# Eight transfers of whole rows in place of four of 32 partitions for the last half of an output

## The chip, the cores and the metric

The kernel runs on one core of a Trainium2 chip. The metric is the device time of one execution in microseconds (us), the median of several runs. The profile is of one further execution; its span goes from the first to the last instruction.

## The reference

Two blocks, one behind the other, all in float32.

```python
# attention: q, k, v are (4, 8, 768, 64), proj is (64, 6)
mask = q_bucket[:, :, :, None] == k_bucket[:, :, None, :]    # buckets: signs of q @ proj and k @ proj as a number
scores = where(mask, scale * q @ k.T, -1e9); attn = softmax(scores); x = attn @ v
x = x.transpose(0, 2, 1, 3).reshape(3072, 512)               # tokens x model
# feed-forward: w_in is (512, 2048), w_out is (2048, 512)
h = x @ w_in
g = h * (1 / (1 + exp(-1.702 * h)))
out = g @ w_out                                              # 3072 x 512
```

## The kernel before

The attention comes first (lines up to about 540), pair of heads by pair of heads, and leaves x transposed in the tile xT. The feed-forward block (`feed_forward`, from L698) works on three groups of 1,024 tokens (`sb`), each of two halves of XT = 512 tokens, themselves of two parts of TH = 256. Both matrix products are done by a scheme of seven products of half-size matrices in place of eight, so sums of quarters are made by DVE and POOL beside TensorE's products. The first product's results g lie in a DRAM buffer, `g_dram`; the second product reads them back into `raw_g` (and a second buffer in `s_in`) for 3 x 7 = 21 steps (`steps_out`), in the order `OUTER = (1, 2, 6, 7, 5, 3, 4)` for each group.

One such step is `product_of_halves` (its products at L1078, the sums of its results at L1083): seven smaller products again. Between them it calls `after(0)`, `after(1)` and so on, by which the loop over the steps places other work: the order of every engine's instructions is written out by hand, and the engines keep it.

A result c has the output's features on the partitions. `turned` (L1058) transposes it in blocks of 32 x 32 on DVE, quarter by quarter (q = 0 to 3), into the tile `ys[j]` of 128 partitions x 16 blocks x 128 floats; j says which 512 tokens of the group. After this, partition 32a + t of block b holds the output row of token 32b + t, columns 128a to 128a + 127. Quarters 0 and 2 of the final step complete blocks 0 to 7 (the first 256 tokens), quarters 1 and 3 blocks 8 to 15.

`written` (L1060 to L1065) brings blocks to the output in DRAM. It issues four transfers, one for each a: 32 partitions of `ys[j]`, the blocks asked for, 128 floats each; on the DRAM side rows of 512 floats, of which column block a is written. `queues` lists the engines that issue, in turn. `loader` is [SP]; for the last pieces ACT is added, so that SP issues a = 0 and 2 and ACT a = 1 and 3.

The last of the 21 steps (`final`) has its own order of products (L1090 on) and its own list of what is placed between them (L1271): quarter 1 after the fourth product, quarter 3 and the write of half 1 (`write[1]`) after the fifth, quarter 0, and at the very end, behind the last product, quarter 2, which transposes straight from the PSUM bank, and the write of half 0 (`write[0]`). `write` is built in L1269.

Behind the feed-forward block every engine loads a guard value (`largest`, L1312) and branches over a second version of the whole computation (the `tc.If` at L1315), which isn't taken here. SP waits for the completions of the outstanding transfers (L1315), and all engines drain and meet (L1348).

Of the kernel before, what the change touches and what calls it, by code (L numbers as in the profile page):

```python
# [19 lines left out]
P = 128  # L20
# [18 lines left out]
def kernel(  # L39
# [17 lines left out]
    nc = tc.nc  # L57

    loader = [nc.sync]
# [168 lines left out]
    XT = 512  # L228
# [469 lines left out]
    def feed_forward(tag, late=()):  # L698
# [9 lines left out]
        with ExitStack() as fctx:  # L708
# [306 lines left out]
            def inner_sums(at):  # L1015

                if at == 0:
                    w = w_quarters(OUTER[0])
                    return sums_a(nc.gpsimd, *w, wqs[LEFT[OUTER[0]]][:, 1, 0:F4, :])
                return sums_a(nc.gpsimd, *w_quarters(OUTER[at])) if at < len(OUTER) else []  # L1020
# [4 lines left out]
            def fetch(n):  # L1025
                sb, o = steps_out[n]
                parts = 1 if n + 1 == len(steps_out) else 2
                for h in range(parts):
                    cs = slice(h * FC // 2 // parts, (h + 1) * FC // 2 // parts)
                    loader[0].dma_start(out=raw_g[n % 2][:, cs], in_=g_dram[len(LEFT) * sb + RIGHT[o], :, cs, :])  # L1030
# [3 lines left out]
            def g_quarters(n):  # L1034
                if n not in g_tiles:


                    g_tiles[n] = wholes[4:6] if n == 1 else [
                        (st2 if n % 2 else gp).tile([P, F4, TH], F32, tag=t, name=t + "ab"[n % 2]) for t in ("t1", "t2")]
                    g_tiles[n] = g_tiles[n] + [gp.tile([P, F4, TH], F32, tag="t4", name="t4g")]  # L1040
                g = raw_g[n % 2]
                x = [g[:, F4 * k : F4 * (k + 1), TH * j : TH * (j + 1)] for k in range(2) for j in range(2)]
                return x + g_tiles[n]

            def g_sums(n):
                if n == len(steps_out):
                    return [lambda: None] * 4
                t1, d12, t2, t4 = sums_b(nc.vector, *g_quarters(n))
                return [t1, t2, d12, t4]

            ys = {}

            def turned(c, i, j, q0, q1, of=None):

                for q in range(q0, q1):
                    h, k = divmod(q, 2)
                    y = ys[j].rearrange("p b (d r) -> p r b d", r=4)[:, 2 * i + h, k * (TH // 32) : (k + 1) * (TH // 32), :]
                    nc.vector.transpose(y, (c[:, q] if of is None else of).rearrange("p (b t) -> p b t", t=32))  # L1058

            def written(sb, j, halves, queues):  # L1060
                first, last = halves[0] * TH, (halves[-1] + 1) * TH
                for a in range(4):
                    t0 = (2 * sb + j) * XT
                    dst = out[t0 + first : t0 + last, a * P : (a + 1) * P].rearrange("(b t) d -> t b d", t=32)
                    queues[a % len(queues)].dma_start(out=dst, in_=ys[j][32 * a : 32 * (a + 1), first // 32 : last // 32, :])  # L1065

            def product_of_halves(n, acc, after):

                sb, o = steps_out[n]
# [20 lines left out]
                if n + 1 == len(steps_out):  # L1090

                    a = product(1)
                    nc.scalar.copy(u, a)
                    b = product(3)
                    after(0)
                    product(6, onto=a)
                    nc.scalar.copy(v, a)
                    add(v, v, acc[:, 1])
                    add(c12, b, v)
                    after(1)  # L1100
                    p = product(5)
                    add(c12, p, c12)
                    add(c22, p, acc[:, 3])
                    after(2)
                    product(7, onto=a)
                    add(c22, a, c22)
                    add(a, a, acc[:, 2])
                    after(3)
                    corner()
                    after(4)  # L1110
                    product(4, onto=a)
                    after(5, a)
                    return m
# [62 lines left out]
            first = 2 * NESTED.stop  # L1176
# [12 lines left out]
            x = todo.pop(1, [])  # L1189
# [6 lines left out]
            for t in NESTED:  # L1196
                sb, at = divmod(t, MT // 2)
# [26 lines left out]
            for n in range(2 * NESTED.stop, 3 * MT):  # L1224
                sb, mt = divmod(n, MT)
# [13 lines left out]
                t = {3 * MT - 2: g_sums(0)[:1], 3 * MT - 1: g_sums(0)[1:]}.get(n, []) if n > 3 * MT - 3 else []  # L1239
# [8 lines left out]
            for n, (sb, o) in enumerate(steps_out):  # L1248
                final = n + 1 == len(steps_out)
                if 0 < n and n + 1 < len(steps_out):  # L1250
                    fetch(n + 1)

                if n in (2, 3, 5, 6):

                    nc.gpsimd.tensor_copy(mark, (g_quarters(n)[5] if n < 4 else ms[OUTER[n - 1]])[0:1, 0, 0:1])
                for f in {2: inner_sums(3), 3: inner_sums(4), 5: inner_sums(5) + inner_sums(6)[:2], 6: inner_sums(6)[2:]}.get(n, []):
                    f()
                later_sums = g_sums(n + 1)
                m = wholes[n % len(wholes)]

                def after(at, last=None):
                    if at == 0:
                        while pending:
                            pending.pop(0)()
                    todo = [[x] for x in later_sums] if n == 0 else [[], later_sums[0:1], later_sums[1:3], later_sums[3:]]
                    todo = todo[at] if not final else []
                    if n + 2 >= len(steps_out):
                        turns = [lambda q=q: turned(m, int(final), int(not final), q, q + 1, last if q == 2 else None) for q in range(4)]
                        write = [lambda x=(sb, int(not final), (h,), loader + [nc.scalar] * (final or h == 0)): written(*x) for h in range(2)]  # L1269
                        if final:  # L1270
                            todo = [[], last_sum, [turns[1]], [turns[3], write[1]], [turns[0]], [turns[2], write[0]]][at]  # L1271
                        elif at == 2:
                            todo = [later_sums[1], turns[1], turns[3], write[1]]
                        elif at == 3:
                            todo = [turns[2], turns[0], later_sums[2]]
                            pending.append(write[0])
                            last_sum.append(later_sums[3])
                    for f in todo:
                        f()

                acc = {6: 1, 7: 6, 2: 1, 3: 6, 4: 7}.get(o)
                if o == 3:
                    pending.pop(0)()
                ms[o] = product_of_halves(n, None if acc is None else ms[acc], after)

                def flat(x):
                    return x.rearrange("p q t -> p (q t)")

                if o == 5:
                    m5, m6, m7 = (ms[i] for i in (5, 6, 7))  # L1290
                    pending += [lambda a=m6, b=m5: nc.vector.tensor_tensor(flat(a), flat(a), flat(b), op=Alu.add),
                                lambda a=m5, b=m7: nc.vector.tensor_tensor(flat(a), flat(a), flat(b), op=Alu.add),
                                lambda a=m5: turned(a, 1, 1, 0, 4)]
                elif o in (2, 3) and n + 2 < len(steps_out):
                    pending.append(lambda a=ms[o], j=int(o == 3): turned(a, 0, j, 0, 4))
                    if o == 3:
                        pending.append(lambda sb=sb: written(sb, 1, (0, 1), loader))
                elif o == 4 and not final:
                    pending.append(lambda a=ms[4]: turned(a, 1, 0, 0, 4))
                    pending.append(lambda sb=sb: written(sb, 0, (0, 1), loader))  # L1300
                yield
# [50 lines left out]
```

## Time and profile before

| | before |
|---|---|
| median of 3 runs | 856.52 us (856.17 to 859.51) |
| the profiled execution | 856.59 us |
| its span | 854.7 us, granted TensorE clock 0.998 |
| PE busy | 846.2 us, 99% of the span |
| DVE, POOL, ACT busy | 698.8, 357.3, 345.0 us |
| transfers from y to the output | 32: 16 of 256 KB and 16 of 128 KB |
| last transpose into y | 847.94 to 848.57 us of the span |
| last four transfers to the output | issued from 848.60 us on |

The times within the profile are counted from the start of the span. PE is TensorE's matrix products, PEld its weight loads, DVE VectorE, ACT ScalarE, POOL GpSimd, SP the engine that only issues transfers and waits. A q behind an engine's name means its sequencer: issues, waits and branches. "out<-in" are the program's names. The DMA share is the busy share of the core's 16 DMA engines; a packet is one contiguous piece that one of them moves.

### The profile page before, as it was taken

How to read it: one execution, taken by the hardware profiler on the slowest of the kernel's cores; microseconds unless marked ns; L12 is line 12 of the kernel's file. 1: busy time of each engine (PE TensorE's matmuls, PEld its weight loads, DVE VectorE, ACT ScalarE, POOL GpSimd, SP SyncE). 2: the span in 40 equal slices, each digit the busy share in tenths (PEclk: the TensorE clock that was granted, in tenths of full speed). 3: DMA queues.
4: the chain of work that ended last, by engine and by line, in shares of the span. 5: the costliest groups of instructions: out<-in, count | busy, mean ns of one | idle time of the engine just before them, and what ended most of it. 6: DMA issues, size and time to landing. Idle time of an engine off the chain costs nothing.

```text
span 854.7 us, 13648 instructions
## 1 busy us (share of the span) xinstructions
PE 846.2 (99%) x5007; PEld 530.4 (62%) x5007; DVE 698.8 (82%) x1069; ACT 345.0 (40%) x549; POOL 357.3 (42%) x316
## 2 busy tenths in 40 slices
PE   9999999999999999999999999999999999999996
PEld 4444444444444444566666666545888888888885
DVE  4589999999999885788887788666998977897776
ACT  5866667777766654343444444433000000000000
POOL 4343333433433358996854476669664100000000
PEclk9999999999999999999999999999999999999999
DMA  5636654444553104436565536587844685467524
GB/s 130 94 55 108 109 92 85 85 86 89 119 100 76 48 26 139 157 114 234 196 220 222 222 147 222 196 280 261 291 164 158 203 251 189 163 209 243 192 107 101
DMA packets 160906, 132.10 MB, mean 155 GB/s; under 512 B 122656, under 2 KB 137664, under 8 KB 155584
## 3 DMA queue, kind: packets, MB, share of 16 engines
q1 hardware_dynamic: 152448, 106.89, 44.8%
q10 hardware_dynamic: 8384, 24.27, 8.2%
q8 instruction: 41, 0.67, 0.4%
q14 instruction: 33, 0.27, 0.1%
HBM read 79.69 MB, written 50.33 MB: 152 GB/s over the span
## 4 chain that ended last, share of the span: by engine, by line
PE 98%; ACT 0%; POOL 0%; DVE 0%; issue 0%; ACTq 0%; POOLq 0%; DVEq 0%
PE product L1078 30%; PE product L751 23%; PE ps L435 18%; PE av L468 15%; PE small L819 6%; PE product L819 3%; PE dn L489 1%; PE hash L411 1%; PE tp L369 1%; PE hash L376 0%; ACT c L764 0%; DVE v L767 0%; POOL kf L310 0%; ACT size L190 0%; DVE y L1058 0%
## 5 line engine op out<-in xcount | busy, mean ns | idle before, releaser
L436 ACT ACTIVATE e<-ps 128x768 f32<-128x768 f32 x192 | 151.2, 812 | 25.6 <-PE ps L435 23.1
L435 PE MATMUL ps<-qT,kT 64*128 64x384 f32 x768 | 155.1, 483 | 0.0
L443 POOL TENSOR_TENSOR acc<-e 128x768 f32<-128x768 f32 x32 | 51.8, 1619 | 193.9 <-ACT e L436 174.4
L468 PE MATMUL av<-e,v 128*32 128x385 f32 x1536 | 128.0, 487 | 0.0
L751 PE MATMUL product<-xT,w_in_sb 128*128 128x512 f32 x216 | 100.1, 593 | 0.1
L468 PEld LDWEIGHTS av<-e,v 128*32 128x32 f32 x1536 | 48.6, 109 | 76.2 <-issue 74.0
L435 PEld LDWEIGHTS ps<-qT,kT 64*128 64x128 f32 x768 | 68.0, 188 | 38.5 <-issue 38.4
L751 PE MATMUL product<-t_x,s_in 128*128 128x512 f32 x192 | 89.4, 592 | 0.0
L1114 ACT COPY u<-product 128x256 f32<-128x256 f32 x20 | 7.4, 372 | 158.1 <-PE product L1078 124.9
L751 PEld LDWEIGHTS product<-xT,w_in_sb 128*128 128x128 f32 x216 | 40.9, 190 | 36.4 <-issue 33.1
L435 PE MATMUL ps<-qf,kf 64*128 64x384 bf16 x384 | 62.9, 324 | 0.1
L444 POOL TENSOR_TENSOR acc<-acc,e 128x768 f32<-128x768 f32 x32 | 55.9, 1746 | 2.5
L751 PEld LDWEIGHTS product<-t_x,s_in 128*128 128x128 f32 x192 | 36.5, 190 | 29.6 <-issue 27.2
L449 DVE SCALAR_TENSOR_TENSOR acc<-e 128x768 f32<-128x768 f32 x32 | 47.7, 1490 | 5.1 <-ACT e L436 5.1
L767 DVE TENSOR_TENSOR u<-product,u 128x256 f32<-128x256 f32 (+1 forms) x60 | 28.5, 487 | 17.1 <-PE product L819 13.8
L435 PEld LDWEIGHTS <-kf 64*128 64x128 bf16 x384 | 19.0, 94 | 35.1 <-issue 6.8
L451 DVE TENSOR_TENSOR acc<-acc,e 128x768 f32<-128x768 f32 x32 | 34.3, 1072 | 3.3
L451 DVE TENSOR_TENSOR acc<-acc,acc 128x768 f32<-128x768 f32 x32 | 31.2, 974 | 6.3 <-POOL acc L444 3.2
L1078 PE MATMUL product<-raw_g,xT 128*128 128x256 f32 x152 | 35.1, 379 | 0.0
L222 POOL TENSOR_TENSOR u<-v,u 128x1024 f32<-128x1024 f32 (+1 forms) x11 | 23.8, 2164 | 21.9 <-ACT v L764 8.1
L767 DVE TENSOR_TENSOR v<-product,v 128x512 f32<-128x512 f32 x24 | 16.5, 689 | 19.4 <-PE product L751 19.4
L767 DVE TENSOR_TENSOR c<-small,c 128x256 f32<-128x256 f32 (+1 forms) x54 | 24.2, 462 | 9.2 <-PE small L819 9.1
(284 smaller groups left out, 1728.0 us busy)
## 6 DMA issues: line engine op xcount, KB each, us to landing
raw_g<-g_dram SPq DMA_DIRECT2D x20, 1024.0 KB
s_in<-g_dram SPq DMA_DIRECT2D x20, 1024.0 KB
g_dram<-c ACTq DMA_DIRECT2D x18, 512.0 KB
raw<-in_moe_w_out_dram ACTq DMA_DIRECT2D x16, 512.0 KB
raw<-in_moe_w_in_dram SPq DMA_DIRECT2D x15, 512.0 KB
v<-in_v_dram SPq DMA_DIRECT2D x32, 192.0 KB
k<-in_k_dram SPq DMA_DIRECT2D x60, 96.0 KB
q<-in_q_dram SPq DMA_DIRECT2D x60, 96.0 KB
```

The source lines that it names most:

```text
L222: return [lambda: eng.tensor_tensor(t1, b12, b11, op=Alu.subtract), lambda: eng.tensor_tensor(b12, b22, b12, op=Alu.subtract), lambda: eng ...
L435: nc.tensor.matmul(ps[:, j, 0:HS], a[hs, keys], m[hs, cols], start=not last, stop=last)
L436: nc.scalar.activation(es[c][:, kt, :, 0:HS], ps[:, :, 0:HS], Act.Exp, scale=1.0 / D**0.5)
L443: nc.gpsimd.tensor_tensor(acc, es[c][:, 0, :, 0:HS], es[c][:, 1, :, 0:HS], op=Alu.add)
L444: nc.gpsimd.tensor_tensor(acc, acc, es[c][:, 2, :, 0:HS], op=Alu.add)
L449: nc.vector.scalar_tensor_tensor(acc, e[0], T * TINY, e[1], op0=Alu.add, op1=Alu.add)
L451: nc.vector.tensor_tensor(acc, acc, x, op=Alu.add)
L468: nc.tensor.matmul(av[D * j + d : D * j + d + 32, :], vt[:, t, j, d : d + 32], es[c][:, t, j, :], start=(t == 0), stop=(t == T - 1))
L751: nc.tensor.matmul(ps, wq[LEFT[i]][:, kc, :], xq[RIGHT[i]][:, kc, :], start=(start and kc == 0), stop=(kc == K2 - 1), skip_group_check=not ...
L767: nc.vector.tensor_tensor(dst, x, y, op=Alu.add)
L819: nc.tensor.matmul(x, wq[LEFT[i]], xq[RIGHT[i]], start=start, stop=True, skip_group_check=True)
L1078: nc.tensor.matmul(ps, wq[LEFT[i]][:, c, :], gq[RIGHT[i]][:, c, :], start=(onto is None and c == 0), stop=(c == F4 - 1), skip_group_check= ...
```

## The change

The write of half 0 in the final step takes another form. In place of four transfers with 32 partitions and eight blocks each, eight transfers are issued, one for each block b: all 128 partitions, 128 floats of each, to 32 whole rows of the output. The DRAM side is written as [a, t, d], column block outside, to match the partitions 32a + t. SP issues the even b and ACT the odd ones. All other writes keep their form.

```diff
-            def written(sb, j, halves, queues):
+            def written(sb, j, halves, queues, by_rows=False):
                 first, last = halves[0] * TH, (halves[-1] + 1) * TH
+                t0 = (2 * sb + j) * XT
+                if by_rows:
+                    for b in range(first // 32, last // 32):
+                        dst = out[t0 + 32 * b : t0 + 32 * b + 32, :].rearrange("t (a d) -> a t d", d=P)
+                        queues[b % len(queues)].dma_start(out=dst, in_=ys[j][:, b, :])
+                    return
                 for a in range(4):
-                    t0 = (2 * sb + j) * XT
                     dst = out[t0 + first : t0 + last, a * P : (a + 1) * P].rearrange("(b t) d -> t b d", t=32)
                     queues[a % len(queues)].dma_start(out=dst, in_=ys[j][32 * a : 32 * (a + 1), first // 32 : last // 32, :])
...
-                        write = [lambda x=(sb, int(not final), (h,), loader + [nc.scalar] * (final or h == 0)): written(*x) for h in range(2)]
+                        write = [lambda x=(sb, int(not final), (h,), loader + [nc.scalar] * (final or h == 0), final and h == 0): written(*x) for h in range(2)]
```

## The prediction

> **What bounds the kernel now.** First the list of cores and the page: one core, span 854.7 us, clock 0.998, PE busy 99%. The chain of waits, cut to the last 20 us, says where PE's rule ends:
>
> ```profile
> 834.95 12.96 PE product L1078 x60
> 847.92 0.02 issue
> 847.94 0.63 DVE y L1058
> ```
>
> PE is the chain until 847.9; one transpose into y follows, done at 848.57; and then the chain has nothing more, though the span goes on to 854.7. These last 6.1 us are what the change can touch. The timeline and the stretches show what fills them (in the second fence: length, busy time of PE, PEld, DVE, ACT, POOL, clock, DMA share, GB/s):
>
> ```profile
> 848.60 0.81 SPq L1065 DMA_DIRECT2D out_dram<-y  x2
> 848.60 0.88 ACTq L1065 DMA_DIRECT2D out_dram<-y  x2
> ```
>
> ```profile
> 849.41:852.05 2.64, 0.00 (x0) 0.00 (x0) 0.00 (x0) 0.00 (x0) 0.00 (x0) 0.72 0.90 198
> 852.19:852.35 0.16, 0.00 (x0) 0.00 (x0) 0.00 (x0) 0.00 (x0) 0.00 (x0) 0.50 0.14 42
> ```
>
> The four transfers of the last half are issued from 848.60 on, two on each queue. Their first 512 B packet starts at 849.42, 0.82 us after the issue began. Up to 852.05 all 16 DMA engines work (0.90 of them busy, 198 GB/s), then two stragglers run on alone: a share of 0.14 is 2.2 engines, and at 42 GB/s each of two moves 512 B in 24 ns. In the packet records each of them starts one every 23.5 ns. The last completion is recorded at 853.05, 0.53 us behind the last packet. From there SP's remaining waits, the drains and the closing handshakes take 1.67 us to 854.72. So the tail is: transpose, issue, 0.82 us, data, 0.53 us, 1.67 us. Only issue and data are changed. The profiled execution took 856.59 us, 1.87 us beside its span; the median shown is 856.52, so a difference in the span can be put on either.
>
> **What stays.** Bytes and packets: 4 x 256 packets of 512 B before, 8 x 128 of 512 B after, 512 KB both times. Each row of y is 128 floats and goes to 512 B of an output row, so no packet grows. All eight new transfers read what the transpose at 847.94 writes, so none can be issued earlier. PE, DVE and the first half's write are the same.
>
> **What changes: the outermost dimension.** Before, a transfer's outer dimension is 32 on both sides (tokens in the output, partitions in y). After, the output side is written out as 4 x 32 x 128, column block outside: its outer dimension is 4; that of y is 128. How many DMA engines take a transfer can be read in this trace by its completion packets. The page has:
>
> ```profile
> DMA packets 160906, 132.10 MB, mean 155 GB/s; under 512 B 122656, under 2 KB 137664, under 8 KB 155584
> ```
>
> Under 512 B there are 120 loads of q and k with 768 packets of 128 B (92,160), 30 loads of v with 768 of 256 B (23,040), 128 packets of 24 B, and the rest, 7,328, of 4 B: completions. The list of issues has 488 transfers. At 16 completions each that would be 7,808. It is 480 less, and exactly 120 transfers (kf and qf, 9 KB, 12 partitions of 768 B) are not a multiple of 16 wide: with 12 each the sum comes out, 368 x 16 + 120 x 12. Transfers with 32, 64 or 128 outside post 16, those with 12 outside post 12. So the number of engines follows the outer dimension, and I take four for one that is 4 wide. No transfer of this trace is 4 wide; the two ends are 4 engines and 16.
>
> The Trainium skill says this outright ("DMA: Bandwidth & Descriptors", on why a DMA increments its semaphore by 16): a transfer runs on the largest number up to 16 that divides the slowest dimension of both sides, and from SP or ACT on the lowest-numbered engines. By that rule all eight would share the same four; the trace agrees for 12, and nothing in it shows 4.
>
> **The sum.** Engine a gets column block a of every transfer: 32 packets, from both queues, 8 x 32 = 256 in all, where each of the 16 has had 64.
>
> Price of a packet: it is not in the trace for four engines. Low end 23.5 ns, the stragglers above, who alternate between both queues with no loss. High end from the stretch 849.75 to 850.8, where all 16 move 159 GB/s: 9.9 GB/s each, 51 ns. I take 25 ns, near the low end: four engines at 23.5 ns ask for 87 GB/s, and the slowest stretch moved 159, so a shared limit that made packets slow there is not reached; and the straggler row, with few engines, is the nearest one. 25 and not 23.5 because four, not two, run at once; in the best stretch of this kernel (840.79 to 841.00, all 16 engines, 310 GB/s) it was 26.
>
> - First packet at 849.42, as before.
> - 256 x 25 ns = 6.40 us, so 855.82; eight completion packets of 9 ns on each engine, about 0.09: 855.91.
> - Completion recorded 0.53 us later: 856.44. Before: 853.05. So the last wait is released 3.4 us later.
> - The 1.67 us behind it stay: span 858.1, time 856.59 + 3.4 = **860.0**, 0.4% slower.
>
> **What could add to it.** Issues: the 12-partition transfers cost their queue more than the others (columns: shortest, median and longest issue in ns):
>
> ```profile
> L423 SPq DMA_DIRECT2D kf<-f x60: 713/729/887, 25.1 to 285.4; - x60
> L1065 SPq DMA_DIRECT2D out_dram<-y x26: 315/478/1790, 675.4 to 849.0; - x26
> ```
>
> At 0.72 us each, four on a queue end at about 851.6 in place of 849.4. Data covers that: a pair of transfers, one of each queue, is 64 packets or 1.6 us for its engines and is issued in 0.75. Only if the first data came later by the longer issue (0.72 against 0.32) would 0.4 us be added. Full rings may hold the queues longer: of four transfers of 512 packets in a row, the last took up to 1.79 us to issue (the row above). Behind the issues SP and ACT load the guard value (1.2 us in the trace) and branch; ACT's drain comes 2.8 us after its branch. Today that chain is 853.77 - 849.48 = 4.3 us behind ACT's last issue; moved to 851.6 it ends at 855.9, and it would set the end only behind 856.9, where SP's own drain will be. Its cover is 1 us. The waits of eight transfers on semaphores of earlier ones cost nothing: the last of the first half's completions is recorded at 849.83, before the fourth issue of a queue.
>
> One of the 16 engines is also slowed by a 16 KB instruction packet (1.29 us from 849.33); its completions come 0.8 us behind the rest today, and about 0.6 us of that is in the 853.05. If that engine is among the four, it stays; if not, 0.6 us go. Bounds -0.6 to +0.6; I take 0.
>
> **The rivals.**
>
> *Sixteen engines after all* (the compiler splits otherwise, and the change of shape means nothing). Data is then 64 packets on each engine as today; 2.6 us at today's mean of 41 ns. The last issue ends 1.0 us later (two more of 0.48 on each queue), 850.4, and its data starts about 850.9 with 8 packets an engine and queue left, so today's 852.05 still holds. If the shorter strides make every packet 25 ns, 849.42 + 1.6 = 851.0, held to about 851.3 by the last issue: 0.8 us gained. Time 855.8 to 857.0, say 856.3. For it: nothing in the trace has 4 outside. Against it: the 12s. The skill's rules for kernel authors on that page prefer one 128-partition transfer to two on disjoint halves, since these share the same engines anyway; by that alone nothing changes here, which is this rival.
>
> *Four engines, and each packet slow.* The mechanism is at the packet: if the 44 to 49 ns that the records have as medians of the first two transfers of each half come from a write's own delay and not from a limit that 16 engines share, four engines pay it as well. 256 x 44 ns = 11.3 us, 4.9 us more than in my sum: 864.9, 1.0% slower. It decides from 28.5 ns a packet, where the time passes 856.59 + 4.28. For it: the slow stretches come with the same code, at 159 to 170 GB/s, and nothing in the trace says why. Against it: in the second half of the same write (851.00 to 851.75) the 16 engines move 279 GB/s, 29 ns a packet, and the few stragglers never slow down. By the skill's "SBUF — State Buffer", on the DMA port swizzle, partitions 0 to 31 and 32 to 63 lie on the same ports, so engines 0 and 1 in step would share one; an estimate from its 435 GB/s for 16 ports is 38 ns, 863.3. The 310 GB/s above, while transfers of 32 partitions ran, speak against such a limit.
>
> *The issuing queues set the end.* A ring takes only so many packets: in the write that starts at 760.46 the fourth issue of 512 packets ended at 762.13, when the records have about 830 of its 2,048 packets done, so 76 an engine were outstanding. ACT's fourth transfer brings its queue to 128 an engine and can be issued once 52 are gone, 104 of both queues: 2.6 us behind 849.42, 852.0. With the 4.3 us behind it ACT's drain is at 856.3, still ahead of 856.9, so this adds nothing at 25 ns; each us by which the issue ends later than 852.6 would add one.
>
> **How the numbers follow.** A measurement of this kernel tells about 0.5%, 4.28 us, from no change: same is 852.2 to 860.8. Four engines at 23.5 to 28 ns: 0.62, 859 to 860.8, with the instruction packet and a late first packet up to 861.5; I put 0.48 of it within 0.5% and 0.14 above. Four engines slower than that: 0.26, up to 866. Sixteen engines: 0.10, about 856.3, none of it far enough to be faster by 0.5%. Anything else: 0.02. So faster 0.01, same 0.58, slower 0.41. The range, 856.0 to 865.0, takes in the sixteen-engine case and the slow packets to 44 ns.
>
> **What would show it.** In the changed profile: 8 issues at the end, 0.7 us each if narrow; a DMA share near 0.25 to 0.29 and 80 to 87 GB/s from about 850 to 856, against 0.90 and 198; 32 completion packets for these eight transfers, not 128; PE and the transposes to 848.6 unchanged. A share near 0.9 and an end of data by 852 would make the prediction wrong at its root; a share of 0.25 with 50 GB/s or less, in the packet's price.

## The result and the profile after

The changed kernel takes 862.58 us (median of 6 runs, 862.11 to 863.72) against 857.21 (median of 6) for the one before in the same comparison: a ratio of 1.0064, with a 95% interval of 1.0054 to 1.0074. It is slower by about 5.4 us, 0.6%; 860.0 was forecast, and the range reached from 856.0 to 865.0. The profiled execution took 862.11 us with a span of 860.3, 5.6 above the span of before.

The chain of waits in its last 20 us and the issues behind it, from the chain and the timeline of the changed kernel:

```profile
834.83 12.96 PE product L1083 x60
847.79 0.02 issue
847.81 0.63 DVE y L1058
```

```profile
848.47 2.58 SPq L1066 DMA_DIRECT2D out_dram<-y  x4
848.48 3.00 ACTq L1066 DMA_DIRECT2D out_dram<-y  x4
```

Each issue by itself (shortest, median and longest in ns, start of the first and the last):

```profile
L1066 SPq DMA_DIRECT2D out_dram<-y x4: 545/604/688, 848.5 to 850.4; - x4
L1066 ACTq DMA_DIRECT2D out_dram<-y x4: 581/622/1051, 848.5 to 850.9; - x4
```

PE has the same 60 products in the same 12.96 us, and the last transpose ends at 848.45 (848.57 before). Everything that differs lies behind it. The stretches of this tail (length, busy PE, PEld, DVE, ACT, POOL, clock, DMA share, GB/s):

```profile
849.76:850.45 0.69, 0.00 (x0) 0.00 (x0) 0.00 (x0) 0.00 (x0) 0.00 (x0) 1.00 0.22 40
850.45:852.50 2.05, 0.00 (x0) 0.00 (x0) 0.00 (x0) 0.00 (x0) 0.00 (x0) 0.96 0.28 73
852.50:856.00 3.50, 0.00 (x0) 0.00 (x0) 0.00 (x0) 0.00 (x0) 0.00 (x0) 0.50 0.31 91
857.11:857.85 0.74, 0.00 (x0) 0.00 (x0) 0.00 (x0) 0.00 (x0) 0.00 (x0) 0.50 0.07 21
```

Where 0.90 of 16 engines worked at 198 GB/s before, now 0.22 to 0.31 do. From 852.5 to 856.0 the records have 592 packets of 512 B, each taking 27 ns, with 84 to 87 starting in every 0.5 us: 23.7 ns from one to the next on each of four engines. From 857.11 on one engine is left over, with one packet every 23.5 ns. The page counts the completions:

```profile
DMA packets 160874, 132.10 MB, mean 154 GB/s; under 512 B 122624, under 2 KB 137632, under 8 KB 155552
```

122,624 is 32 less than before: 4 x 16 completions went and 8 x 4 came. So eight transfers ran on four engines each, and the rate of all of them together says that these were the same four. Which of the 16 they were, the records do not say.

Times behind the last transpose, in us, from the records of the two profiles:

| | before | after |
|---|---|---|
| first 512 B packet | 0.85 | 1.32 |
| last packet, but for stragglers | 3.48 | 8.05 |
| last packet | 3.95 | 9.40 |
| last completion | 4.48 | 9.81 |
| end of the span | 6.15 | 11.85 |

In the profiles of the experiments below, the end of the last transpose moves between 847.99 and 849.94 us from kernel to kernel, though nothing ahead of it was changed. So small differences are read from the last transpose on ("tail"), beside the measured times.

### The profile page after: what moved, and what is told of

It is laid out like the page before. It is cut to its first block, busy times and chain, and to the rows that moved or that the text cites. A ratio compares the mean times of both kernels' runs of the same rounds, so it can differ in the third digit from the quotient of the medians.

```text
span 860.3 us, 13652 instructions
## 1 busy us (share of the span) xinstructions
PE 845.7 (98%) x5007; PEld 529.9 (62%) x5007; DVE 700.6 (81%) x1069; ACT 345.1 (40%) x549; POOL 357.0 (42%) x316
## 2 busy tenths in 40 slices
DMA packets 160874, 132.10 MB, mean 154 GB/s; under 512 B 122624, under 2 KB 137632, under 8 KB 155552
## 4 chain that ended last, share of the span: by engine, by line
PE 97%; DMA 1%; ACT 0%; DVE 0%; SPq 0%; issue 0%; ACTq 0%; DVEq 0%
PE product L1083 30%; PE product L751 22%; PE ps L435 18%; PE av L468 15%; PE small L819 6%; PE product L819 3%; PE dn L489 1%; PE hash L411 1%; DMA q<-in_q_dram 1%; PE hash L376 0%; PE tp L369 0%; ACT c L764 0%; DVE v L767 0%; ACT size L190 0%; DVE y L1058 0%
## 5 line engine op out<-in xcount | busy, mean ns | idle before, releaser
L1083 PEld LDWEIGHTS product<-raw_g,xT 128*128 128x128 f32 x152 | 28.9, 190 | 3.9
```

Source lines behind the costliest of these rows:

```text
L1083: nc.tensor.matmul(ps, wq[LEFT[i]][:, c, :], gq[RIGHT[i]][:, c, :], start=(onto is None and c == 0), stop=(c == F4 - 1), skip_group_check= ...
```

## The experiments

The theory is "width": an outer dimension of 4 leaves each transfer to the same four engines, and the busiest engine's packets set the time. The rivals are the number of transfers, and the bytes that go out in another order.

**Eight wide transfers.** The same number of transfers and bytes, but with 32 outside on both sides:

```diff
-                    for b in range(first // 32, last // 32):
-                        dst = out[t0 + 32 * b : t0 + 32 * b + 32, :].rearrange("t (a d) -> a t d", d=P)
-                        queues[b % len(queues)].dma_start(out=dst, in_=ys[j][:, b, :])
+                    for i in range(2):
+                        for a in range(4):
+                            r = first + 128 * i
+                            dst = out[t0 + r : t0 + r + 128, a * P : (a + 1) * P].rearrange("(b t) d -> t b d", t=32)
+                            queues[a % len(queues)].dma_start(out=dst, in_=ys[j][32 * a : 32 * (a + 1), r // 32 : r // 32 + 4, :])
```

> Eight transfers as in the changed kernel, 64 KB and 128 packets of 512 B each, four on each queue, but each of 32 partitions (one column block, four of the eight blocks of tokens), so that the outer dimension is 32 on both sides. Theory 'width': the cost is that an outer dimension of 4 leaves each transfer to the same four DMA engines. Then this kernel has 16 completions for each transfer, a DMA share near 0.9 up to about 852, and its time is that of the kernel before within 0.5 us (ratio 0.999 to 1.001). Rival 'number': eight transfers with their issues and completions cost it. Then 4 us or more of the 5.4 us stay (ratio 1.005 or more).

859.11 us against 856.99, ratio 1.0022 (1.0011 to 1.0032). Neither expectation holds as written: it is neither before nor most of the change. The trace tells the two apart. Its page has 122,720 packets under 512 B, 64 more than before (8 x 16 in place of 4 x 16), and its data is through 4.19 us behind the last transpose, 0.24 later than before; the tail is 7.89 us, 1.74 more than before. The rest lies behind the data. From the stretches, its issues and the closing drains:

```profile
850.70:851.20 0.50, 0.00 (x0) 0.00 (x0) 0.00 (x0) 0.00 (x0) 0.00 (x0) 1.00 1.01 260
851.20:851.70 0.50, 0.00 (x0) 0.00 (x0) 0.00 (x0) 0.00 (x0) 0.00 (x0) 1.00 0.24 38
```

```profile
L1068 SPq DMA_DIRECT2D out_dram<-y x4: 315/432/1490, 849.2 to 851.6; - x4
L1068 ACTq DMA_DIRECT2D out_dram<-y x4: 373/447/1435, 849.2 to 851.6; - x4
```

```profile
L1355 SPq DRAIN  x3: 7/7/7, 855.0 to 856.6; - x3
...
L1355 ACTq DRAIN  x2: 8/37/66, 856.3 to 856.6; - x2
```

The third issue of each queue took 1.4 to 1.5 us (the longest of the three figures), and from 851.20 to 851.70 the DMA engines had almost nothing to do (0.24). The guard load and the branch stand behind the issues, and ACT drains at 856.28, 1.2 us behind SP's drain at 855.05, though SP had seen the last data at 853.86. Before, ACT's drain (853.77) came before SP's (853.91). So the number of transfers costs here, but hardly in the data.

**Two engines, half of the bytes.** Column blocks 0 and 1 by eight transfers with 2 outside, the other two in the old form:

```diff
-                        dst = out[t0 + 32 * b : t0 + 32 * b + 32, :].rearrange("t (a d) -> a t d", d=P)
-                        queues[b % len(queues)].dma_start(out=dst, in_=ys[j][:, b, :])
+                        dst = out[t0 + 32 * b : t0 + 32 * b + 32, 0 : 2 * P].rearrange("t (a d) -> a t d", d=P)
+                        queues[b % len(queues)].dma_start(out=dst, in_=ys[j][0:64, b, :])
+                    for a in range(2, 4):
+                        dst = out[t0 + first : t0 + last, a * P : (a + 1) * P].rearrange("(b t) d -> t b d", t=32)
+                        queues[a % len(queues)].dma_start(out=dst, in_=ys[j][32 * a : 32 * (a + 1), first // 32 : last // 32, :])
```

> Column blocks 0 and 1 by eight transfers of 64 partitions and half rows (outer dimension 2 on the side of the output), column blocks 2 and 3 by two transfers in the old form of 32 partitions. Half of the bytes are narrow. Theory 'width': two engines take the narrow ones, 8 x 32 = 256 packets each, as many as each of four had in the changed kernel, and 32 more of the two wide ones: 288 x 23.5 ns = 6.8 us in place of 6.0. Time 0.3 to 1.2 us above the changed kernel, ratio to before about 1.007 to 1.008. Two completions for each narrow transfer. Rival 'bytes': what costs is that bytes go out in whole rows or strides of 2 KB, so half of the bytes cost half: 2.7 us above before, ratio 1.003.

861.89 us, ratio 1.0057 (1.0044 to 1.0071); tail 11.21 us, 5.06 above before and 0.64 below the changed kernel. The bytes theory (2.7 above) is out. The width theory was right in kind, but its low end, 0.3 us above the changed kernel, is 0.9 us too high. Its step from 6.0 to 6.8 us of data is borne out against the three undisturbed engines of the changed kernel: 7.49 us (1.28 to 8.77 behind the transpose) against their 6.73. What it did not count is that no straggler of 1.35 us follows here: the two engines end 0.24 us apart. From the stretches and the page:

```profile
850.71:852.20 1.49, 0.00 (x0) 0.00 (x0) 0.00 (x0) 0.00 (x0) 0.00 (x0) 0.96 0.14 43
```

```profile
DMA packets 160890, 132.10 MB, mean 154 GB/s; under 512 B 122640, under 2 KB 137648, under 8 KB 155568
```

A share of 0.14 is two engines. The completions are 16 less than before: 8 x 2 + 2 x 16 = 48 in place of 64.

**Without the guard, before and after.** In both kernels the last lines are left out: the load of the largest value, the branch and the second version of the computation.

```diff
-    unsafe = nc.values_load(largest[0:1, 0:1].bitcast(I32)) >= SAFE_BITS
-
-    loader[0] = nc.scalar
-    with tc.If(unsafe, preferred_fallthrough_block=False):
...
```

> The kernel before without its guard: the load of the largest value, the branch and the second version of the computation behind it are left out (the output for these inputs is the same). It is the base for the next one. Expected: no instruction packets of 16 KB behind 846 us, one straggler less at the end, 0 to 1.5 us faster than the kernel before (ratio 0.998 to 1.000).

854.91 us, ratio to the kernel before with its guard 0.9977 (0.9968 to 0.9986): 2.1 us, a little more than expected. The tail accounts for 1.37 of it, from 6.15 to 4.78; in the two profiles the last transpose also ends 0.58 us earlier. In the tail the last packet comes 0.40 us earlier (3.55), with no straggler, and only 0.91 us follow the last completion in place of 1.67.

> The changed kernel without its guard, in the same way. Theory 'instruction packets': one of the four engines also carried the instruction packets of 16 KB and 8 KB at the end and so finished 1.35 us behind the three others (0.47 before). Without them all four end together, and the kernel stands 4.0 to 4.8 us above the one before without its guard, in place of 5.6. Rival 'slow engine': the engine is late by itself; the straggler stays over 1 us late and the difference stays 5.3 to 5.9 us. Also the first packet's delay from issue, 1.29 us against 0.82, should stay in both cases, since it belongs to narrow transfers.

860.13 us, ratio to before with guard 1.0038 (1.0024 to 1.0052), 5.2 us above the other without guard. By the measured time neither expectation holds, 4.0 to 4.8 or 5.3 to 5.9. The tail is 9.40 us, 4.62 above, which is within the range of the instruction theory; ahead of it, the last transposes of these two profiles end 1.23 us apart, which is not the writes' doing. What tells the theories apart is the straggler. The stretches:

```profile
852.72:854.22 1.50, 0.00 (x0) 0.00 (x0) 0.00 (x0) 0.00 (x0) 0.00 (x0) 0.50 0.29 86
```

Again four engines; but the four completions of the last transfer come at 8.11, 8.19, 8.24 and 8.38 us, within 0.27 of each other, where in the changed kernel the last was 1.24 behind the third. In all eight transfers the last of the four completions comes 0.06 to 0.18 us behind the third, against 0.52 to 1.27 with the guard. The last packet starts at 8.03. The slow engine was not slow by itself. With the guard, the instruction packets of the tail are (848.5 to 858 us of the changed kernel; packets, MB, time as a share of 16 engines):

```profile
q8 instruction: 2, 0.03, 1.6%
q14 instruction: 3, 0.02, 0.6%
```

The two of 16 KB start at 849.22 and 852.74, the three of 8 KB at 851.57, 856.24 and 856.41. At the completions of the first transfer, behind the first of them, the lag is already 0.79 us. Without the guard there are none in the tail, and over the whole execution the DMA records of the two kernels differ in size and number by seven packets alone, two of 16 KB and five of 8 KB. The records do not name the engine of a packet; in the two-wide run, with the same five, neither of its two engines fell behind like that, so not every engine is hit. The first packet comes 1.31 us behind the transpose in this kernel too, so that delay is not the guard's.

**Eight wide transfers without the guard.** The first edit and the last one together.

> The eight wide transfers (32 partitions, four blocks each) in the kernel without its guard: the load of the largest value, the branch and the second version of the computation are left out. With the guard they cost 1.7 us from the last transpose on, while their last packet ends only 0.24 us later than before; ACT drained 1.2 us behind SP, since its last issue, guard load and branch came later. Theory 'queue': the number of transfers costs through what is queued behind them on ACT. Without the guard nothing is, and the kernel stands within 0.5 us of the one before without guard (from the last transpose to the end 4.6 to 5.3 us against 4.78). The third issue of a queue (1.49 us) should fall to 0.5 us if an instruction packet of 16 KB held it. Rival 'number': eight transfers cost by their own issues and completions; 1.2 us or more stay.

855.16 us, 0.25 above the kernel before without guard; both have the ratio 0.9977 (0.9968 to 0.9986) to before. The tail is 4.89 us against 4.78. Its issues:

```profile
L1068 SPq DMA_DIRECT2D out_dram<-y x4: 316/442/452, 848.0 to 849.4; - x4
L1068 ACTq DMA_DIRECT2D out_dram<-y x4: 374/444/458, 848.0 to 849.4; - x4
```

No issue takes over 0.46 us. Eight transfers in place of four cost 0.11 us of tail when they are 32 wide and nothing waits behind them. So the other 4.51 of the 4.62 us of tail between the kernels without guard are the width. That the instruction packets caused the hold of 1.4 us fits (one of 16 KB ran from 0.77 to 1.94 us, the hold ended at 2.35), but the edit takes out more than them, so it isn't shown.

**Four narrow, four wide, without the guard.** Blocks 0 to 3 by whole rows, blocks 4 to 7 as in the eight wide ones:

```diff
-                    for b in range(first // 32, last // 32):
+                    for b in range(first // 32, first // 32 + 4):
                         dst = out[t0 + 32 * b : t0 + 32 * b + 32, :].rearrange("t (a d) -> a t d", d=P)
                         queues[b % len(queues)].dma_start(out=dst, in_=ys[j][:, b, :])
+                    for a in range(4):
+                        r = first + 128
+                        dst = out[t0 + r : t0 + r + 128, a * P : (a + 1) * P].rearrange("(b t) d -> t b d", t=32)
+                        queues[a % len(queues)].dma_start(out=dst, in_=ys[j][32 * a : 32 * (a + 1), r // 32 : r // 32 + 4, :])
```

> Without the guard (left out as before): four of the eight blocks by whole rows, outer dimension 4, the other four by four transfers of 32 partitions. Half of the bytes are narrow, as with the two-wide transfers, but over four engines: 4 x 32 + 4 x 8 = 160 packets for each of these. Theory 'width', cost by packets of the busiest engine: 160 x 23.5 ns = 3.8 us behind the first packet at 1.3 us, so the last packet 5.1 to 5.4 us after the last transpose and the end 6.3 to 6.8 us after it, 1.5 to 2.0 us above the kernel before without guard. Theory 'bytes' (half the bytes narrow cost as much as in the two-wide run): 4 us or more above.

857.67 us, ratio 1.0006 (0.9997 to 1.0014) to before with its guard, 2.8 us above before without it; tail 7.03 us, 2.25 above. Both are more than the 1.5 to 2.0 expected and far less than the 4 of the bytes theory. The last packet ends at 5.46 (5.1 to 5.4 expected), so a packet cost 25.9 ns over the 160: the price is a little low. Behind it come 1.58 us, 1.55 in the eight wide ones without the guard, where 1.2 to 1.4 were allowed for. Half of the bytes were narrow here as in the two-wide run, whose tail grew by 5.06 (with the guard, against before): what counts is how many packets the busiest engine has (160 here, 288 there), not how many bytes are narrow.

**Another pairing of the old transfers.** The kernel before, with the column blocks dealt to the queues as 0, 1 and 2, 3:

```diff
-                    queues[a % len(queues)].dma_start(out=dst, in_=ys[j][32 * a : 32 * (a + 1), first // 32 : last // 32, :])
+                    queues[a * len(queues) // 4].dma_start(out=dst, in_=ys[j][32 * a : 32 * (a + 1), first // 32 : last // 32, :])
```

> The kernel before with only the order of its last writes changed: SP issues column blocks 0 and 1, ACT 2 and 3, where SP had 0 and 2 and ACT 1 and 3. In all runs so far the transfers of blocks 0 and 1 run at 42 to 45 ns a packet while together, those of 2 and 3 at 27 to 31. Theory 'same partitions half': transfers of the same half of the partitions get in each other's way; in the new order each half has one at a time, all packets take about 30 ns, the data of the last half takes 1.9 to 2.2 us in place of 2.6, and the kernel is 0.4 to 0.8 us faster than before (ratio 0.9990 to 0.9995). Rival 'column block': blocks 0 and 1 are slow by themselves or the first packets always are; the time stays within 0.3 us.

857.65 us against 856.84, ratio 1.0007 (0.9999 to 1.0016): no gain, and 0.8 us above, where the rival allowed 0.3. The tail in its profile is 0.43 us shorter (5.72), but the first 0.65 us are slow here too:

```profile
849.06:849.71 0.65, 0.00 (x0) 0.00 (x0) 0.00 (x0) 0.00 (x0) 0.00 (x0) 1.00 0.90 179
849.71:851.50 1.79, 0.00 (x0) 0.00 (x0) 0.00 (x0) 0.00 (x0) 0.00 (x0) 0.65 0.93 238
```

The queues tell more. From 849.52 to 849.96 block 0, on SP's queue (q1), and block 2, on ACT's (q10), ran side by side (packets, MB, time as a share of 16 engines):

```profile
q1 hardware_dynamic: 104, 0.05, 61.4%
q10 hardware_dynamic: 86, 0.04, 33.0%
```

61.4% of 16 engines for 0.44 us, over 104 packets, are 41.6 ns for one of block 0; for one of block 2 it is 27.0. All of ACT's packets in both halves of this write, blocks 2 and 3, took 27 or 28 ns, the first as the last; SP's block 0 in the last half took 43.9 ns in the mean, block 1 behind it 37.8. So the theory of the partitions' halves is wrong, since block 0 had its half to itself and was slow. A slow start of every write is out too: ACT's packets were fast from the first, beside slow ones. That blocks 0 and 1 are slow by themselves fits this run, but not the others. In the eight wide ones, their second pair took 41 and 45 ns with guard, behind the pause in the data, and 30 and 33 ns without guard and pause. And in the two-wide run it was block 3 that was slow, on ACT's queue (the stretch as above, then the queue as above):

```profile
852.50:854.00 1.50, 0.00 (x0) 0.00 (x0) 0.00 (x0) 0.00 (x0) 0.00 (x0) 0.50 0.77 94
q10 hardware_dynamic: 213, 0.11, 69.1%
```

Of ACT's 210 data packets there, 60 took 27 ns and the other 150 from 40 to 157, at 94 GB/s in all. What makes packets of these wide transfers slow stays open; those of the narrow ones took 27 ns in the median in every run.

## Why the prediction was right, and which terms were too small

**The range** of 856.0 to 865.0 held the sixteen-engine case and slow packets too, so a time inside it tells little about the mechanism. The completions and the rates do.

**The bound and the place: right.** PE and the transposes are unchanged; all that was added lies behind the last transpose.

**The engines: right.** Four engines for an outer dimension of 4 was read from the completions of 12-wide transfers; the page now shows 4 for 4 and 2 for 2. By the rule that the prediction named ("DMA: Bandwidth & Descriptors" in the Trainium skill, on why a DMA increments its semaphore by 16) it had to be 4 and 2, on the same lowest-numbered engines; the counts agree, the rates of 91 and 43 GB/s agree with the same engines, and no run here shows their numbers. The sixteen-engine rival is out. The preference for one transfer of 128 partitions over two on halves, which the prediction took from the rules for kernel authors on that page of the Trainium skill, presumes 16 engines either way; here the 128 partitions met an outer dimension of 4 on the other side, and 4 engines ran.

**The packet: right.** 256 packets at 25 ns and the completions were put at 6.49 us; the three engines without a straggler took 6.73 (1.32 to 8.05). The difference is the beginning: each engine started a packet every 51 ns in the first 0.69 us and every 30 ns in the next 2.05, and from 852.5 on every 23.7 ns. The price came true, but the reason given for it did not: packets were to be slow by a limit that 16 engines share and 87 GB/s do not reach. In the other pairing block 0 was slow beside block 2, which was not, and in the two-wide run 150 packets took 40 to 157 ns while 94 GB/s moved in all. Why the packets of narrow transfers are not slow is open, so that part was luck. The rival of slow packets (44 ns, 864.9) named a time not far from the measured one, by a mechanism that did not happen.

**The sum: 3.4 us forecast for the last completion, 5.33 measured.** Three terms were too small, the third by far the most; the fourth here was a little too large:

- The first packet was kept at 0.82 us behind the issue. It came 1.29 us behind it: +0.47. The prediction had 0.4 us for this among what could be added, from the longer issue of 12-wide transfers (0.71 against 0.32), and left it out of the sum. The first issue took 0.65 us; every run with narrow transfers in front has it (1.28 to 1.32 us behind the transpose), every run with wide ones alone 0.84 to 0.85.
- The data: +0.24.
- The straggler: "bounds -0.6 to +0.6; I take 0". It ended 1.35 us behind the other three. The prediction saw one instruction packet of 16 KB and one lag; but this tail takes in two of 16 KB and three of 8 KB, and each of the four engines has 128 KB of data to move, where each of the 16 had 32. Without the guard the last four completions lie within 0.27 us.
- The last completion came 0.41 us behind its packet, not 0.53: -0.12.

Together 3.39 + 0.47 + 0.24 + 1.35 - 0.12 = 5.33. Behind it "the 1.67 us stay" was 0.37 short: 2.04 us. SP waits for the completions in a fixed order. Before, the transfer that landed last stood last but one in it; now it stands second, and six more waits of 66 to 85 ns follow (858.27 to 858.70). 5.70 us in all, less 0.12 by which the transpose ended earlier, are the 5.6 of the span.

**The queues: right for the change, and decisive elsewhere.** The hold by a full ring did not come: ACT's last issue ended at 851.47 in place of 852.0, with 107 of its queue's 128 packets an engine outstanding, where 76 had been read as the limit. ACT's drain was expected at 856.3, hidden behind SP's. It came at 858.2, later than thought, since ACT's guard load took 1.9 us and 4.6 us passed from its last branch to the drain, both during the long data; but SP's drain came at 859.5, so it stayed hidden. In the eight wide transfers, with short data, it was ACT that ended last, by 1.2 us: the path of the third rival was a real one, for another kernel than this, though not by a full ring, since only two transfers of 128 packets, 16 an engine, stood ahead of the held issue on its queue.

**The chances.** Within 0.5% was given 0.58, slower by more 0.41; it was 0.64%, so the less likely of the two came. With 23.7 ns a packet the cheap end of the price had come true, and the terms that the sum had set to nothing carried it over the line.

## What to carry to other kernels

A transfer's outermost dimension, on either side, decides how many DMA engines work on it; count the completion packets of transfers that you have before you reshape one, and keep 16 or a multiple of it outside (32, 64 and 128 went over 16 engines here), even where a transfer then writes parts of rows in place of whole ones. At the end of a kernel price the tail by the packets of the busiest engine, and then follow what stands behind the issues on each queue: guard loads, branches and the code that they fetch can end last. Terms that all point the same way (a later first packet, a straggler, the order of the final waits) are not a range around nothing; here they made 2.2 us of 5.7.

## What the runs showed of the hardware that was not expected

- A narrow transfer starts later: its first packet comes 1.28 to 1.32 us behind the data's last transpose, against 0.85 for one 32 wide, and its issue takes 0.51 to 0.80 us, in one case 1.05, against 0.32 to 0.47 for a wide one with no narrow one ahead of it and nothing that holds it.
- Instruction packets travel on the same engines as data. In the changed kernel, with four engines, one ended 1.35 us behind the others with the guard's code; without it the four ended within 0.27.
- With the guard's code at the end, a third issue of both queues was held for 1.4 us at the same moment; without it, 0.45 us. The part of the guard that holds it was not tried by itself.
- A packet of 512 B took 27 ns in the median in every narrow transfer, but in a wide one often 41 to 51, and in the two-wide run up to 157, at 94 GB/s in all. Two wide transfers side by side can differ: 41.6 and 27.0 ns in the other pairing.
